# Attention and gated feed-forward on one core: the front as one pinned list of small steps, with the scaling of eight weight conversions on GpSimd

## The chip, the cores and the metric

The kernel runs on one core of a Trainium2 chip. The metric is the device time of one execution in microseconds (us), the median of several runs. TensorE is called PE in the profile (PEld is its weight load), VectorE DVE, ScalarE ACT, GpSimd POOL, and SP is the engine that issues nearly all transfers.

## The reference

```
scores = q @ k.T / sqrt(D);  mask: key at most 63 positions back, none ahead
attn   = exp(scores - max); attn /= (sum + 1e-9)
x      = (attn @ v)   as [4608 tokens, 512]
out    = (sigmoid(x @ w_gate) * (x @ w_val)) @ w_out
```

There are 8 sequences of 576 tokens with 8 heads of 64. The weights are 512x1536, 512x1536 and 1536x512. All is computed to float32 accuracy; the weights arrive as 64-bit numbers, and every product is split in a high and a low part (float32r), three matmuls for one.

## The kernel before

**Tiles.** The 4608 tokens are 12 tiles of 384. A unit of attention is (t, p): tile t and one of 4 pairs of heads p. The hidden width is 12 groups j of 128. Tiles 0 and 1 are computed group by group as the weights come in; tiles 2 to 11 use a scheme with seven products for eight (`product`, `last_product`) and read sums of the weights that are stored to device memory on the way.

**The front.** Before the up-projection of tiles 0 and 1 can run densely, their eight attention units have to be done, since a matmul of the up-projection runs over all four pairs. A unit is: load of q, k (`load_qk`) and v (`load_v`); `scores` (24 matmuls into two PSUM banks, one for each head h of the pair); `softmax`, for each h three pieces u: a DVE operation that adds the mask, scales, negates and finds the lowest value (L249), an exponential on ACT (L257), for h = 0 with a sum in a second ACT instruction; for h = 1 a sum on DVE (L270); then 2(sum + 1e-9) (L264) and its reciprocal (L265) on DVE, and the multiplication by it on GpSimd (L274, 128x384); `stage_b`: three transposes for each h on TensorE (L328) and a copy on ACT (L333); `stage_c`: 24 matmuls with v (L358), high part on ACT (L365), low part on DVE (L366). Then `up_gate` and `up_val` (12 matmuls each, L394), tanh on ACT (L402), the product (L407) and its split on DVE (L420, L422), `down` (L442).

**Weight conversion.** Conversion i is group j = i // 3 of matrix m = i % 3 (gate, val, out). `conv_load` brings 128x512 64-bit numbers (512 KB) to one of six `raw` buffers. `conv_a` scales the high words and the low words, two operations on ACT over every second 32-bit word (L117, L118), the one to a `w32` tile (three buffers), the other in place. `conv_b` puts the float32 together, three operations on DVE (L126, L128, L130). `conv_c` rounds the high part on ACT (L158), takes the low part on DVE (L159), stores parts for the later scheme (`put_part`, `wo_parts`) and the whole `w32` tile (`w32d`).

**Order.** Each piece of work is put into `events` with a time worked out by hand (`put(time, rank, function, ...)`); the events are sorted and traced in that order. The order of the instructions of an engine is then fixed at build time by a scheduler with its own timing; TensorE's keeps the traced order (`pe`). `tc.issue_after(x)` puts an instruction behind x on its engine; conversions use it with `marks` (the last copies of units, the split of a group). Tiles of one tag share its buffers, so a new tile waits until an old one has been read. PSUM banks of the up-projection rotate over three (`h_bank`).

Of the kernel before, what the change touches and what calls it, by code (L numbers as in the profile page):

```python
# [26 lines left out]
def attn_ffn(ctx: ExitStack, tc: tile.TileContext, qT, kT, vN, w_gate, w_val, w_out, out, outT):  # L27
# [74 lines left out]
    def conv_load(i):  # L102
        j, m = divmod(i, KINDS)
        raw = mp.tile([P, DM], I64, name=f"raw_{m}_{j}", tag="raw", bufs=RAW)
        marks["conv_load"] = nc.sync.dma_start(out=raw, in_=w_src[m][J_AT[j]]).ins
        conv[i] = raw

    def conv_a(i):

# [7 lines left out]
        nc.scalar.activation(w32, hw, AF.Copy, scale=2.0 ** -112)  # L117
        nc.scalar.activation(r32, lw, AF.Copy, scale=2.0 ** -29)  # L118
        conv[i] = (r32, w32)

    def conv_b(i):
        j, m = divmod(i, KINDS)
# [3 lines left out]
        nc.vector.tensor_scalar(out=zz, in0=wi, scalar1=4, scalar2=1,  # L126
                                op0=ALU.logical_shift_left, op1=ALU.logical_shift_right)
        nc.vector.scalar_tensor_tensor(out=wi, in0=wi, scalar=-2 ** 31, in1=zz,  # L128
                                       op0=ALU.bitwise_and, op1=ALU.bitwise_or)
        nc.vector.tensor_add(out=wi, in0=wi, in1=r32)  # L130

    def conv_c(i):
        j, m = divmod(i, KINDS)
        _, w32 = conv.pop(i)
# [19 lines left out]
        nc.sync.dma_start(out=w32d[m][J], in_=w32)
        marks[("w", i)] = (cp,)

    def split(w32, hi, lo, eng):
        cp = nc.scalar.copy(hi, w32)  # L158
# [67 lines left out]
    def softmax(t, p):  # L229
        sc = sc_of.pop((t, p))  # L230
        for h in range(2):
            exponentials(t, p, h, sc[h])
            normalize(t, p, h)

    def exponentials(t, p, h, sc):
        g0 = order[t] * UT
# [6 lines left out]
        if h == 0:  # L243
            sums_of[(t, p)] = sm.tile([P, 2, UP], F32, name=f"rs_{t}_{p}", tag="rs")
        rs = sums_of[(t, p)][:, h, :]
        for u in range(UP):
# [2 lines left out]
            nc.vector.tensor_tensor_reduce(out=pt[:, u, :], in0=sc[u], in1=masks[key],  # L249
                                           op0=ALU.add, op1=ALU.min, scale=-SCALE, scalar=3.0e38,  # L250
                                           accum_out=mn[:, u:u + 1])
            with ExitStack() as behind:
                behind.enter_context(table_order())
                if NP * t + p - 2 in marks["pT"] and (t, p) != (1, NP - 1):
                    behind.enter_context(tc.issue_after(marks["pT"][NP * t + p - 2]))
# [1 line left out]
                exp = nc.scalar.activation(pt[:, u, :], pt[:, u, :], AF.Exp, bias=mn[:, u:u + 1],  # L257
                                           scale=-1.0, **sums)
            chain.append(exp.ins)
        st[(t, p, h)] = pt  # L260

    def invert(rs):

        nc.vector.scalar_tensor_tensor(out=rs, in0=rs, scalar=2e-9, in1=rs, op0=ALU.add, op1=ALU.add)  # L264
        nc.vector.reciprocal(out=rs, in_=rs)  # L265

    def normalize(t, p, h):
        pt, rs = st[(t, p, h)], sums_of[(t, p)][:, h, :]
        if t < 2 and h:
            nc.vector.reduce_sum(out=rs, in_=pt, axis=mybir.AxisListType.X)  # L270
# [51 lines left out]

    def stage_b(t, p):
        for h in range(2):
            pt = st[(t, p, h)]
            pp = bank(t, p, f"p{h}", f"pp{h}_{t}_{p}")
            for u in range(UP):
                pe(nc.tensor.transpose(pp[:, u, :], pt[:, u, :], ident))  # L328
            if t < 2:
                pT = mp.tile([P, TT], F32, name=f"pT{h}_{t}_{p}", tag="g", bufs=4).rearrange("p (u c) -> p u c", u=UP)  # L330
            else:
                pT = pt
            cp = nc.scalar.copy(pT, pp)  # L333
            marks["pTv"] = cp.ins
# [27 lines left out]

    def x_split(src, nm, i, eng):
        x2 = xp.tile([P, 2, TT], F32R, name=f"x_{nm}", tag=f"x{i}")
        hi = nc.scalar.copy(x2[:, 0, :], src)  # L365
        lo = eng.tensor_sub(out=x2[:, 1, :], in0=src, in1=x2[:, 0, :].bitcast(F32))  # L366
# [653 lines left out]
```

## Time and profile before

| | |
|---|---|
| median of 3 runs | 947.2 us (946.29 to 947.6) |
| span of the profiled execution, first to last instruction | 945.2 us |
| what the median of the runs has beyond this span | 2.0 us |
| PE busy | 930.8 us, 98% |
| DVE busy | 713.7 us, 76% |
| ACT busy | 501.7 us, 53% |
| POOL busy | 151.2 us, 16% |
| transfers | 273.45 MB, mean 289 GB/s |

The profiled execution is one execution on the chip; its own time is given as the span, so sums are made against that. A row of the timeline gives start, duration, engine, line, operation, output and inputs with shapes, and count; brackets give the idle time in front and what ended it. A group row gives busy time and the mean of one in ns; a source row minimum, median and maximum in ns.

### The profile page before, as it was taken

Reading aid. Unit: us, or ns where it says so; the run is one execution under the profiler, and the core shown is the slowest. Engines: PE = TensorE matmul, PEld = TensorE weight load, DVE = VectorE, ACT = ScalarE, POOL = GpSimd, SP = SyncE. Lnnn points to the kernel's source line nnn. Section 1 sums busy time; section 2 is a strip of 40 time slices with the busy share of each in tenths; the row PEclk is TensorE's granted clock in tenths of the full one; section 3 lists DMA queues with packets and bytes.
Section 4 is the critical chain, followed back from the end, with each engine's and each line's share of the span. In section 5 each row is a group of like instructions: output and inputs, shape, how many; then the busy total and the mean of one; then the engine's idle time right before and its main releaser. Section 6 shows DMA issues by size and latency. Waiting matters only on the chain.

```text
span 945.2 us, 20293 instructions
## 1 busy us (share of the span) xinstructions
PE 930.8 (98%) x7164; PEld 897.2 (95%) x7164; DVE 713.7 (76%) x1919; ACT 501.7 (53%) x1374; POOL 151.2 (16%) x232
## 2 busy tenths in 40 slices
PE   6999999999999999999999999999999999999998
PEld 5899999889999999999999999999999999999998
DVE  7999989887888975666885676796567796566882
ACT  7867676655666653545653255564155555222450
POOL 4201104605683000311100013100011100000000
PEclk9999999999999999999999999999999999999999
DMA  9899998989999989888879888889888688988364
GB/s 339 309 386 366 359 320 283 358 295 352 388 321 314 405 284 294 288 273 270 269 251 312 264 283 293 270 244 288 284 278 280 213 246 281 297 251 256 128 222 158
DMA packets 105509, 273.45 MB, mean 289 GB/s; under 512 B 11456, under 2 KB 33600, under 8 KB 105408
## 3 DMA queue, kind: packets, MB, share of 16 engines
q1 hardware_dynamic: 105408, 272.15, 85.2%
q8 instruction: 57, 0.93, 0.4%
q14 instruction: 44, 0.36, 0.1%
HBM read 220.20 MB, written 51.90 MB: 288 GB/s over the span
## 4 chain that ended last, share of the span: by engine, by line
PE 95%; DVE 2%; DMA 1%; ACT 0%; issue 0%; DVEq 0%; ACTq 0%
PE pr L619 46%; PE y L619 23%; PE ph L394 10%; PE y L442 5%; PE pp L328 3%; PE pr L358 2%; PE s L224 1%; PE oo L358 1%; PE pr L224 1%; DMA wt<-wd 1%; PE s L358 1%; DVE p L249 0%; DVE rs L264 0%; ACT p L257 0%; DVE x L366 0%; DVE rs L270 0%
## 5 line engine op out<-in xcount | busy, mean ns | idle before, releaser
L619 PE MATMUL pr<-x_T,wt 128*128 128x384 f32 x1224 | 224.5, 335 | 0.0
L619 PE MATMUL y<-h,wot 128*128 128x384 f32 x1260 | 219.9, 334 | 0.0
L619 PEld LDWEIGHTS y<-h,wot 128*128 128x128 f32 x1260 | 218.3, 188 | 0.7 <-DVE h L407 0.6
L619 PEld LDWEIGHTS pr<-x_T,wt 128*128 128x128 f32 x1224 | 212.6, 188 | 0.3 <-issue 0.3
L619 PE MATMUL pr<-x_B,wt 128*128 128x384 f32 x1008 | 188.6, 337 | 1.0 <-DMA wt<-wd 1.0
L619 PEld LDWEIGHTS pr<-x_B,wt 128*128 128x128 f32 x1008 | 174.6, 188 | 3.5 <-issue 2.1
L701 ACT CAST h<-h 128x384 fp32r<-128x384 f32 x210 | 104.3, 514 | 91.7 <-PE y L619 41.1
L274 POOL TENSOR_TENSOR p<-p,rs 128x384 f32<-128x384 f32 x76 | 69.3, 926 | 521.7 <-DVE rs L265 243.3
L702 DVE TENSOR_TENSOR h<-h,h 128x384 fp32r<-128x384 f32 x210 | 111.7, 559 | 22.0 <-ACT h L701 21.5
L257 ACT ACTIVATE p<-p,mn 128x128 f32<-128x128 f32 x288 | 110.8, 392 | 20.5 <-DVE mn L249 20.2
L402 ACT ACTIVATE g<-c 128x384 f32<-128x384 f32 x90 | 47.0, 522 | 117.7 <-DVE c L658 117.5
L394 PE MATMUL ph<-x,w 128*128 128x384 f32 x576 | 106.0, 338 | 0.1
L394 PEld LDWEIGHTS ph<-x,w 128*128 128x128 f32 x576 | 99.8, 188 | 2.5 <-issue 0.9
L629 DVE TENSOR_TENSOR c<-pr,p 128x384 f32<-128x384 f32 x60 | 33.0, 550 | 44.5 <-PE pr L619 44.5
L407 DVE SCALAR_TENSOR_TENSOR h<-g,c 128x384 f32<-128x384 f32 x90 | 50.3, 559 | 6.2 <-DVE c L658 0.5
L257 ACT ACTIVATION_READ_ACCUMULATOR p<-p,mn 128x1 f32 x264 | 49.6, 188 | 0.0
L333 ACT COPY p<-pp 128x384 f32<-128x384 f32 x80 | 34.3, 479 | 25.9 <-PE pp L328 23.1
L634 ACT COPY p<-pr 128x384 f32<-128x384 f32 x60 | 27.2, 473 | 37.0 <-PE pr L619 36.9
L629 DVE TENSOR_TENSOR u<-pr,p 128x384 f32<-128x384 f32 x60 | 33.1, 551 | 17.6 <-PE pr L619 17.6
L328 PE MATMUL pp<-ident,p 128*128 128x128 f32 x288 | 41.8, 280 | 2.0 <-POOL p L274 1.9
L619 PE MATMUL pr<-x_T,ws 128*128 128x384 f32 x216 | 40.4, 339 | 0.0
L658 DVE TENSOR_TENSOR c<-pr,p 128x384 f32<-128x384 f32 x60 | 32.9, 554 | 9.6 <-PE pr L619 9.1
(186 smaller groups left out, 1212.1 us busy)
## 6 DMA issues: line engine op xcount, KB each, us to landing
wt<-wd SPq DMA_DIRECT2D x186, 512.0 KB, 4.5
wot<-wod SPq DMA_DIRECT2D x105, 512.0 KB, 4.6
v<-in_vN_dram SPq DMA_DIRECT2D x48, 384.0 KB, 5.5
wd<-ws SPq DMA_DIRECT2D x48, 256.0 KB, 4.9
k<-in_kT_dram SPq DMA_DIRECT2D x48, 224.0 KB, 5.5
q<-in_qT_dram SPq DMA_DIRECT2D x48, 192.0 KB, 5.4
w32d<-w SPq DMA_DIRECT2D x36, 256.0 KB, 4.9
wd<-w SPq DMA_DIRECT2D x36, 256.0 KB, 5.5
```

The lines of the kernel that those rows point to most:

```text
L257: exp = nc.scalar.activation(pt[:, u, :], pt[:, u, :], AF.Exp, bias=mn[:, u:u + 1], scale=-1.0, **sums)
L274: eng.tensor_mul(out=pt, in0=pt, in1=rs.unsqueeze(2).broadcast_to([P, UP, P]))
L328: pe(nc.tensor.transpose(pp[:, u, :], pt[:, u, :], ident))
L358: pe(nc.tensor.matmul(oo[U // 2][h * BLK:(h + 1) * BLK, U % 2 * BLK:(U % 2 + 1) * BLK], vt[:, U, h * BLK:(h + 1) * BLK], pT[h][:, U // 2, ...
L394: pe(nc.tensor.matmul(ph, l, r, start=i == 0, stop=i == len(prs) - 1))
L402: act = nc.scalar.activation(g, c, AF.Tanh)
L407: nc.vector.scalar_tensor_tensor(out=out, in0=g, scalar=1.0, in1=val, op0=ALU.add, op1=ALU.mult)
L442: pe(nc.tensor.matmul(yb[y], l, r, start=first and n == 0, stop=last and n == 2))
L619: pe(nc.tensor.matmul(ps, l, r, start=first and i == 0, stop=last and i == 2, skip_group_check=not check))
L629: marks["plus"] = nc.vector.tensor_add(out=o, in0=ps, in1=a).ins
L701: nc.scalar.copy(h2[:, 0, :], src)
L702: nc.vector.tensor_sub(out=h2[:, 1, :], in0=src, in1=h2[:, 0, :].bitcast(F32))
```

## The change

The functions of the front are cut into steps with names of two letters, each of a few instructions on one engine. A string FRONT lists 333 steps; before all events, they are traced in that order, and every instruction that a step issues through `vector`, `scalar`, `gpsimd` or `sync` keeps its place on its engine. A step that is done is not done again when its event comes (`run`). What is traced for events of a time under 60 is issued behind the last instruction of the list on its engine. The steps: `lq`, `lv`, `cl` loads of q and k, of v, of raw weights; `sc` scores; `tt`, `ex` mask and lowest value, exponential (t.p.h.u); `rd` sum for h = 1; `ia`, `ib` doubled sum, reciprocal; `mu` multiplication; `tr`, `cp` transposes, copy; `ou`, `xh`, `xl` output matmuls, high, low part; `ch`, `cw` scaling of high and low words; `cz`, `cs`, `ca` the three operations of conv_b; `cc`, `cr` high and low part; `ct`, `cd` stores; `ug`, `uv` up-projection matmuls of gate and val; `ut` tanh; `ud` product; `uh`, `ul` its split.

In the list are all eight units, conversions 0 to 7 whole, loads up to conversion 13, loads of units (2,0) and (2,2), both up-projections of (0,0) and (1,0), and the gate matmuls of (0,1). For conversions 0 to 7 `ch` and `cw` run on GpSimd as tensor_scalar; from 8 on they are on ACT as before. The marks that held conversions 0 to 5 behind units are removed.

```
FRONT = """
lq0.0 lq0.1 cl0 lq0.2 sc0.0 lq0.3 cl1 sc0.1 lq1.0 tt0.0.0.2 tt0.0.0.1 ex0.0.0.2 tt0.0.0.0 tt0.0.1.0 ch0 lv0.0
tt0.0.1.2 ex0.0.1.0 tt0.0.1.1 ex0.0.0.0 lq1.1 tt0.1.0.2 cw0 tt0.1.0.0 ex0.0.1.2 tt0.1.0.1 sc0.2 ex0.0.0.1
tt0.1.1.1 tt0.1.1.2 ex0.0.1.1 cl3 ia0.0.0 tt0.1.1.0 ex0.1.1.1 ib0.0.0 cz0 ex0.1.0.0 mu0.0.0 lq1.2 rd0.0.1
sc0.3 ex0.1.0.1 tt0.2.0.0 ex0.1.1.2 ia0.0.1 tt0.2.0.2 ex0.1.1.0 ib0.0.1 tr0.0.0 cs0 ex0.2.0.0 mu0.0.1
ex0.1.0.2 lv0.1 rd0.1.1 ex0.2.0.2 ia0.1.0 tr0.0.1 lv0.3 tt0.2.0.1 cp0.0.0 ib0.1.0 ia0.1.1 tt0.2.1.0 mu0.1.0
ex0.2.0.1 tt0.2.1.1 tt0.2.1.2 sc1.0 cp0.0.1 lq1.3 tt0.3.0.1 tt0.3.0.2 ex0.2.1.2 ch1 tt0.3.0.0 ex0.3.0.2 ou0.0
tt0.3.1.2 tt0.3.1.0 ex0.2.1.1 ca0 cw1 lq2.2 ex0.3.1.0 tr0.1.0 ex0.2.1.0 tt0.3.1.1 sc1.1 ib0.1.1 cp0.1.0 cz1
mu0.1.1 tt1.0.0.0 ex0.3.0.0 rd0.2.1 xh0.0 lv0.2 ch3 tt1.1.0.0 ex0.3.0.1 tr0.1.1 tt1.1.0.2 ex0.3.1.1 tt1.0.0.1
cd0 tt1.0.0.2 cp0.1.1 ia0.2.0 ia0.3.0 ia0.2.1 cz3 ex0.3.1.2 ib0.2.0 ex1.0.0.0 cs1 cl4 ou0.1 mu0.2.0 ex1.0.0.1
tt1.0.1.1 ex1.0.0.2 ib0.2.1 tt1.1.0.1 lv1.1 mu0.2.1 ex1.0.1.1 tt1.0.1.2 tr0.2.0 rd0.3.1 xh0.1 lv1.3 cc0
ib0.3.0 ia1.0.0 ia0.3.1 mu0.3.0 tt1.0.1.0 tr0.2.1 cl2 ex1.1.0.0 ib0.3.1 xl0.0 sc1.2 cp0.2.0 lv1.2 cs3 mu0.3.1
cp0.2.1 lv1.0 tr0.3.0 ex1.1.0.2 xl0.1 cw3 ex1.0.1.0 tr0.3.1 tt1.2.0.2 cp0.3.0 tt1.2.0.1 ou0.2 tt1.2.0.0
cp0.3.1 ib1.0.0 ca1 mu1.0.0 ex1.2.0.0 ou0.3 tt1.2.1.0 ex1.1.0.1 cl6 tt1.2.1.2 tt1.2.1.1 ex1.0.1.2 ia1.1.0 cr0
xh0.2 sc1.3 cd1 cw4 ex1.2.0.2 ib1.1.0 ex1.2.0.1 rd1.0.1 tr1.0.0 xh0.3 mu1.1.0 tt1.1.1.0 lq2.0 xl0.2 ex1.2.1.2
cp1.0.0 tt1.1.1.2 ia1.0.1 cc1 ia1.2.0 tt1.3.0.2 ib1.0.1 xl0.3 ug0.0 ex1.2.1.1 mu1.0.1 ex1.2.1.0 tt1.1.1.1
ex1.1.1.0 tt1.3.0.0 ib1.2.0 tr1.1.0 ex1.1.1.1 cl7 cr1 mu1.2.0 ex1.1.1.2 tr1.0.1 uv0.0 ex1.3.0.0 tt1.3.0.1
rd1.1.1 ch4 ex1.3.0.1 rd1.2.1 ex1.3.0.2 cp1.0.1 tt1.3.1.1 ia1.1.1 ia1.3.0 ut0.0 ib1.1.1 ia1.2.1 cz4 mu1.1.1
ex1.3.1.1 ib1.3.0 tt1.3.1.0 ou1.0 cp1.1.0 tt1.3.1.2 ca3 ex1.3.1.0 mu1.3.0 ex1.3.1.2 tr1.1.1 ib1.2.1 cd3
tr1.2.0 rd1.3.1 mu1.2.1 cp1.1.1 tr1.3.0 cl5 ud0.0 xh1.0 cl9 cc3 ia1.3.1 ib1.3.1 tr1.2.1 cs4 mu1.3.1 ct0
cp1.2.0 ou1.1 cp1.2.1 xl1.0 ca4 cw2 tr1.3.1 cp1.3.0 ou1.2 cr3 cp1.3.1 cd4 ch2 xh1.1 ou1.3 cl10 xh1.2 xl1.1 cw6
cz2 xh1.3 xl1.2 ch6 cc4 xl1.3 ug1.0 cs2 cw7 uh0.0 ca2 uv1.0 ut1.0 cz6 cc2 cd2 cr4 ct1 cs6 ch7 ct3 ug0.1 cr2
lv2.0 cw5 ul0.0 ca6 ch5 cz7 cc6 cd6 cz5 cl8 cs7 cl12 cs5 ct2 ud1.0 ca5 ca7 cc5 cr6 cc7 cd7 cr5 cr7 ct5 cd5
lv2.2 ct6 ct4 cl13 cl11 ct7
"""
```

```diff
+    class Pinned:
+        def __init__(self, eng):
+            self.eng = eng
+        def __getattr__(self, op):
+            def call(*a, **k):
+                ins = getattr(self.eng, op)(*a, **k)
+                if pinned[0]:
+                    tc.keep_in_program_order(ins)
+                    ends[ins.ins.engine] = ins.ins
+                return ins
+            return call
+    vector, scalar, gpsimd, sync = (Pinned(e) for e in (nc.vector, nc.scalar, nc.gpsimd, nc.sync))
+    def run(name, *a):
+        if (name,) + a not in taken:
+            taken.add((name,) + a)
+            steps[name](*a)
...
+    def ch(i):
+        w32 = mp.tile([P, DM], F32, name=f"w32_{m}_{j}", tag="w32", bufs=W32)
+        if i < 8:
+            gpsimd.tensor_scalar(out=w32, in0=hw, scalar1=2.0 ** -112, scalar2=None, op0=ALU.mult)
+        else:
+            scalar.activation(w32, hw, AF.Copy, scale=2.0 ** -112)
...
+    def cw(i):
+        if i < 8:
+            gpsimd.tensor_scalar(out=r32, in0=lw, scalar1=2.0 ** -29, scalar2=None, op0=ALU.mult)
+        else:
+            scalar.activation(r32, lw, AF.Copy, scale=2.0 ** -29)
...
     events.sort(key=lambda x: (x[0], x[1]))
+    pinned[0] = True
+    for token in FRONT.split():
+        run(token[:2], *map(int, token[2:].split(".")))
+    pinned[0] = False
     for tm, _, f, a in events:
-        if f in (conv_a, conv_b, conv_c):
-            with ExitStack() as behind:
+        with ExitStack() as behind:
+            for ins in ends.values() if tm < 60 else ():
+                behind.enter_context(tc.issue_after(ins))
+            if f in (conv_a, conv_b, conv_c):
...
-                key = j - AHEAD if m < 2 else j - 1
-                early = {3: ("1_1",), 2: ("1_3",), 4: ("1_3",), 5: ("1_3",)}.get(a[0], (key,))
+                early = (j - AHEAD if m < 2 else j - 1,)
...
-                if a[0] < 2:
-                    behind.enter_context(tc.issue_after(marks["pT"][a[0] + (f is conv_c)]))
```

More of the change, by code (lines that the diff above doesn't have):

```diff
@@ L141, in conv_c @@
             w2 = wo_all[j][:, j % 2]
-        J = J_AT[j]
         if m == 2:
@@ L233, in softmax, with mask_of, lowest @@
             normalize(t, p, h)
-    def exponentials(t, p, h, sc):
-        g0 = order[t] * UT
+    def mask_of(t, u, h):
+        key = [int((order[t] * UT + 2 * u + s) % SEQ == 0) for s in range(2)]
+        return masks[tuple(key[::-1] if h else key)]
+    def lowest(t, p, h):
         if t < 2 and (NP * t + p) % 3 == 2:
@@ L321, in stage_n, with tr, cp @@
             normalize(t, p, h)
+    @step
+    def tr(t, p, h):
+        pt = st[(t, p, h)]
+        pp = pp_of[(t, p, h)] = bank(t, p, f"p{h}", f"pp{h}_{t}_{p}")
+        for u in range(UP):
+            pe(nc.tensor.transpose(pp[:, u, :], pt[:, u, :], ident))
+    @step
+    def cp(t, p, h):
+        pp = pp_of.pop((t, p, h))
+        if t < 2:
+            pT = mp.tile([P, TT], F32, name=f"pT{h}_{t}_{p}", tag="g", bufs=4).rearrange("p (u c) -> p u c", u=UP)
+        else:
+            pT = st[(t, p, h)]
+        marks["pTv"] = scalar.copy(pT, pp).ins
+        if t < 2:
+            marks["pT"][NP * t + p] = marks["pTv"]
+        st[(t, p, h)] = pT
@@ L323, in stage_b @@
     def stage_b(t, p):
         for h in range(2):
[L325 to L334, printed above, removed]
@@ L335, in stage_b, with ou, xh @@
-            if t < 2:
-                marks["pT"][NP * t + p] = cp.ins
-            st[(t, p, h)] = pT
+            run("tr", t, p, h)
+            run("cp", t, p, h)
+    @step
+    def ou(t, p):
+        oo = oo_of[(t, p)] = bank(t, p, "o", f"oo_{t}_{p}")
+        outputs(t, p, [oo[:, u, :] for u in range(UP)])
+    @step
+    def xh(t, p):
+        oo = oo_of[(t, p)].rearrange("p u c -> p (u c)")
+        if t < 2:
+            x2 = xs[(t, p)] = xp.tile([P, 2, TT], F32R, name=f"x_{t}_{p}", tag=f"x{4 * t + p}")
+            marks[f"{t}_{p}"] = (scalar.copy(x2[:, 0, :], oo).ins,)
+        else:
+            marks["xf"] = scalar.copy(xf_tile(t, p), oo).ins
@@ L339, in stage_c, with xl @@
+    @step
+    def xl(t, p):
+        oo = oo_of.pop((t, p)).rearrange("p u c -> p (u c)")
+        x2 = xs[(t, p)]
+        lo = vector.tensor_sub(out=x2[:, 1, :], in0=oo, in1=x2[:, 0, :].bitcast(F32))
+        marks[f"{t}_{p}"] += (lo.ins,)
     def stage_c(t, p):
-        oo = bank(t, p, "o", f"oo_{t}_{p}")
-        outputs(t, p, [oo[:, u, :] for u in range(UP)])
-        oo = oo.rearrange("p u c -> p (u c)")
+        run("ou", t, p)
+        run("xh", t, p)
         if t < 2:
-            xs[(t, p)] = x_split(oo, f"{t}_{p}", 4 * t + p, nc.vector)
-        else:
-            marks["xf"] = nc.scalar.copy(xf_tile(t, p), oo).ins
+            run("xl", t, p)
```

243 lines of the change are left out of this document (169 added, 74 removed).

## The prediction

> **What bounds the kernel now.** I read the page's engine totals first, then busy time by stretch, then what ended TensorE's waits, and last the front in order of time.
>
> ```profile
> span 945.2 us, 20293 instructions
> PE 930.8 (98%) x7164; PEld 897.2 (95%) x7164; DVE 713.7 (76%) x1919; ACT 501.7 (53%) x1374; POOL 151.2 (16%) x232
> 5.60:34.70 29.10, 24.58 (x348) 19.78 (x348) 26.18 (x146) 26.28 (x95) 13.19 (x15) 1.00 1.02 387
> 34.70:40.30 5.60, 4.78 (x86) 3.99 (x85) 4.86 (x11) 4.18 (x10) 0.83 (x1) 1.00 0.60 228
> 40.30:180.00 139.70, 139.70 (x1041) 130.25 (x1040) 129.01 (x323) 98.28 (x248) 34.38 (x49) 1.00 0.96 343
> 40.30 8.79 PE L394 MATMUL ph<-x,w 128*128 128x384 f32 x48
> ```
>
> (Columns of a stretch: its length, then busy us and count of PE, PEld, DVE, ACT, POOL, granted clock, DMA share, GB/s.) TensorE is idle for 14.4 us in all, and from 40.30 to 180 not at all. Only the first 40.3 us can give anything: call D the start of the 48 up-projection matmuls at 40.30 (two for tile 1, group 0, two for tile 0, group 1). Ahead of D both kernels must do the same TensorE work, all eight attention units and both halves of up(0,0); so the gain is 40.30 minus the new D (the start of ug1.0), less any stall that the new order causes behind it. From 5.6 to 34.7 DVE (26.18 of 29.10) and ACT (26.28) are both about 90% busy: two co-bounds, with DMA full as well.
>
> **Does taking work off ACT move the end?** Rows that give start-to-start times, which is what an engine in a row of work pays:
>
> ```profile
> 21.10 0.42 DVE L126 TENSOR_SCALAR zz<-w 128x512 int32<-128x512 int32 x1
> 21.44 0.17 DVE L265 RECIPROCAL rs<-rs 128x3 f32<-128x3 f32 x1
> 21.56 0.69 DVE L128 SCALAR_TENSOR_TENSOR w<-w,zz 128x512 int32<-128x512 int32 x1
> 22.17 0.55 DVE L366 TENSOR_TENSOR x<-oo,x 128x384 fp32r<-128x384 f32 x1
> 22.64 0.85 DVE L130 CUSTOM_DVE_ANT_0 w<-raw,w 128x1024 uint16<-128x1024 uint16 x1
> ...
> 27.38 0.52 DVE L270 TENSOR_REDUCE rs<-p 128x3 f32<-128x384 f32 x1
> 27.82 0.28 DVE L249 CUSTOM_DVE_ANT_0 p<-s,m 128x128 f32<-128x128 f32 x1
> 28.02 0.08 DVE L249 DVE_READ_ACCUMULATOR2_ANT mn<- 128x1 f32 x1
> ...
> 21.54 0.40 ACT L257 ACTIVATE p<-p,mn 128x128 f32<-128x128 f32 x1
> 21.93 0.40 ACT L257 ACTIVATE p<-p,mn 128x128 f32<-128x128 f32 x1
> 18.41 0.61 ACT L158 CAST w<-w 128x512 fp32r<-128x512 f32 x1
> 18.92 0.67 ACT L117 ACTIVATE w<-raw 128x512 f32<-128x512 f32 x1
> 36.65 0.69 ACT L117 ACTIVATE w<-raw 128x512 f32<-128x512 f32 x1
> 37.23 0.66 ACT L118 ACTIVATE raw<-raw 128x512 int32<-128x512 uint32 x1
> 37.79 1.61 ACT L333 COPY pT<-pp 128x384 f32<-128x384 f32 x4
> ```
>
> DVE: tt 0.21 (0.28 long, the next 0.20 to 0.21 behind it), rd 0.44, xl 0.47, cz 0.34, cs, ca and cr 0.61 each, ib 0.1, ia 0.08. ACT: an ex that also sums 0.39, cc 0.51, a pair ch, cw 1.14. Before, three pairs (conversions 0, 1, 3) lie ahead of D on ACT, 3.4 us, one of them at 36.65 in front of the last copies. They go; on ACT alone D could come 3.4 earlier. But DVE gets more: by rd1.3.1, the last sum, the list has cz, cs, ca, cr 4, 3, 3, 2 times where before had 2 each: 2 x 0.34 + 2 x 0.61 = 1.9 more, less one xl (0.47): 1.4 net. So DVE decides, and with it what it shares with GpSimd:
>
> ```profile
> 26.41 0.83 POOL L274 TENSOR_TENSOR p<-p,rs 128x384 f32<-128x384 f32 x1 [1.64 <-DVE rs L265]
> 26.60 0.65 DVE L264 SCALAR_TENSOR_TENSOR rs<-rs 128x3 f32<-128x3 f32 x1
> 21.78 1.16 POOL L274 TENSOR_TENSOR p<-p,rs 128x384 f32<-128x384 f32 x1 [1.97 <-ACT p L257]
> L264 DVE SCALAR_TENSOR_TENSOR rs<-rs x16: 149/162/666, 7.2 to 35.3; 128x3 f32<-128x3 f32 x16
> L264 DVE SCALAR_TENSOR_TENSOR rs<-rs 128x3 f32<-128x3 f32 x16 | 4.5, 280 | 1.0 <-ACT p L257 0.8
> ```
>
> A 0.16 us DVE operation (median) begun under a GpSimd multiply lasts 0.65 and ends with it, at 27.25 against 27.24; the multiply at 21.78 lasts 1.16 instead of 0.83 because cs at 21.56 has the way. So DVE operations with two SBUF inputs (ia, cs, ca, cr) and GpSimd exclude one another; tt, xl (one input in PSUM) and rd pass. Before, this cost L264 4.5 - 16 x 0.16 = 1.9 us. I count cz, which no row shows under a multiply, as excluded too. The short operation needs its 0.16, so it was let in at 27.09, 0.15 before the multiply's end.
>
> The Trainium skill, "SBUF — State Buffer", section "SBUF: two separate sides", calls the shared port pair an exclusive lock held for the full instruction; the trace agrees on the exclusion, but shows the 0.15 of early release.
>
> **Price X of a scaling on GpSimd** (128x512, one input). No row has it. The nearest:
>
> ```profile
> L274 POOL TENSOR_TENSOR p<-p,rs x76: 825/831/1274, 7.8 to 738.1; 128x384 f32<-128x384 f32 x76
> L543 POOL TENSOR_TENSOR sw<-sw,a x24: 448/460/911, 156.0 to 285.3; 128x128 f32<-128x128 f32 x24
> masks.py:199 POOL TENSOR_SCALAR_AFFINE_SELECT ident<-ident 128x128 f32<-128x128 f32 x1 | 0.3, 342 | 0.1
> masks.py:197 POOL MEMSET ident<- 128x128 f32 x1 | 0.2, 204 | 0.1
> L1005 POOL MEMSET const-float32-0.0<- 128x1 f32 x1 | 0.1, 98 | 0.2 <-issue 0.2
> ```
>
> Two inputs: (825 - 448)/256 = 1.47 ns an element over 0.26 fixed, 1.01 us at 512. No input: (204 - 98)/127 = 0.83 ns over 0.10, 0.53. One input lies between: X = 0.8. Upper end 1.37, the 342 ns of 128 elements scaled by four; lower end 0.53.
>
> The Trainium skill, "GPSIMD Engine Reference", section "3.1 Elementwise — side-by-side cycle accounting", has 512 elements at 1.8 cycles each as 769 ns; with 0.77 the walk below would end 0.15 earlier.
>
> **The walk.** Rows for its start and its end:
>
> ```profile
> 5.61 0.29 DVE L249 CUSTOM_DVE_ANT_0 p<-s,m 128x128 f32<-128x128 f32 x1 [2.46 <-PE s L224]
> 6.57 2.84 PE L224 MATMUL s<-k,q 64*64 64x128 f32 x48 [1.11 <-DMA k<-in_kT_dram]
> ...
> 31.01 0.92 PE L358 MATMUL oo<-pT,v 128*64 128x64 f32 x24
> 34.74 0.54 DVE L270 TENSOR_REDUCE rs<-p 128x3 f32<-128x384 f32 x1
> ```
>
> The pinned list fixes each engine's order. Read with GpSimd's steps as posts, it has a pattern: behind a GpSimd step stand DVE steps that pass (tt, rd, ib, xl), and the excluded ones come after them. So I take each GpSimd step and the passing DVE steps side by side, then the excluded DVE steps, let in 0.15 before GpSimd ends. DVE starts at 5.61, when sc0.0 is done.
> - Start: four tt to 6.45. ch0 waits for raw 0, now the third load pair: 1.38 MB, which the front's 363 to 390 GB/s brings by about 7.0; ch0, cw0 to 8.6. tt0.1.* need sc0.1, half of the 48 matmuls at 6.57, so 8.0: a 1.1 us hole behind the sixth tt. DVE at cz0's end 9.8, cs0's 11.5.
> - Unit 1 to 3: mu0.0.1 with rd and ia, 12.8; mu0.1.0 with four tt, 13.7; ch1 with three tt, then ca0, 14.9; cw1, then cz1, 15.9; mu0.1.1, 16.7; ch3 with four tt, then 3 ia, cz3, ib, cs1, 18.7.
> - mu0.2.0 and mu0.2.1 to 20.3; mu0.3.0 then cs3, 21.7; mu0.3.1 with xl0.1, 22.4; cw3 with three tt, then ca1, 23.8; mu1.0.0 with three tt, then cr0, 25.1.
> - cw4 with rd, 25.9; mu1.1.0 with tt, xl, 2 ia and more, 27.5; mu1.0.1 then cr1, 28.6; mu1.2.0, 29.4; ch4, then ia and cz4, 30.8; mu1.1.1 then ca3, 32.1; mu1.3.0 with rd1.3.1, 32.8; mu1.2.1 with ud0.0, then ia, ib, cs4, 34.3; mu1.3.1 to 35.1.
> - Then as in the rows before: tr1.3.1 0.5, cp 0.45, ou1.3 1.0 (24 matmuls, 0.92) with hops of 0.05 to 0.1: 37.4, where ug1.0 starts, its last x half (xh 0.46, xl 0.55: 38.4) being needed only 1.6 later.
>
> So the last rd begins near 32.2 instead of 34.74, and from there to D it is 5.2 instead of 5.56. The walk has no hops between dependent steps of one engine. Calibrated on before: until 34.74 DVE has 48 tt 10.1, 7 rd 3.1, ia and ib 2.7, 5 xl 2.35, two conversions 4.3 = 22.5, 1.9 excluded, 2.9 idle: 27.3 of 29.1, 1.8 in hops. The list mostly puts another step between ia and ib and between cz, cs and ca, so I take a third, 0.6. **D = 38.0, 2.3 earlier.**
>
> **Other parts.** ACT in the list up to xh1.3: 24 ex of 0.39, 24 of 0.29, 16 cp of 0.37, 8 xh of 0.36, three cc of 0.51, one ut of 0.4 = 27.1 from 5.95, so 33.1 against 37.4: covered, by 4 us. Loads: the last v, lv1.0, stands behind 9.5 MB.
>
> ```profile
> w32d<-w SPq DMA_DIRECT2D x4, 256.0 KB, 5.6
> 51.01 2.27 PE L394 MATMUL ph<-x,w 128*128 128x384 f32 x12
> ```
>
> At 387 GB/s after the 1 MB of the first 5.6 us that is 28 us, and ou1.0 stands at about 29; the chain behind it needs 5, so it would bind only past 32. On SP, cd0 is now ahead of cl4 and six v loads, but it is the 26th issue and ca0 is done at 14.9; cd3, behind ca3 at 32.1, holds back cl5 and cl9 alone, which nothing ahead of D uses.
>
> Behind D the list pins conversions 5 to 7 ahead of everything else. ug1.1 (D + 10.7, as 51.01 is to 40.30 now) needs the PSUM bank of uv1.0, freed by ud1.0. On DVE ud1.0 stands behind cs2, uh, ca2, cz6, cr4, cs6, cr2, ul, ca6, cz7, cz5, cs7, cs5: 7.0 from D + 1. But ch5 needs conversion 2's w32 buffer, whose store is issued after ca2 (D + 2.9) and lands 5.6 later (row): ch5 ends at D + 9.3, ud1.0 at D + 11.4, a stall of 0.7; a landing 0.7 sooner, and none. I take 0.2. The removed waits of conversions on marks cost nothing, the list replaces them.
>
> Sum: 40.30 - 38.0 - 0.2 = 2.1 off the profiled span of 945.2, so 943.1; the median stands 2.0 above that span, for what lies around it: 945.1, rounded to **945.0**.
>
> **Rivals.**
> - *GpSimd's price.* X = 1.37 lengthens six groups where the scaling is longer than its cover (ch1, cw1, ch3, cw3, cw4, ch4): from 4.8 to 8.2, D 41.4, 948.5, slower; with X at 1.15 nothing is gained. For it: stride of two words and a uint32 input, in no row. Against: the two-input rate gives 1.01. At 0.53 D comes 0.9 earlier, 944.1.
> - *The bank.* If the w32 store lands 2 us later than its median, in a queue that runs full, the stall is 2.5 and the gain is gone: 947.3.
> - *The port is held to the very end.* Nine groups wait 0.15 more: D 39.4, 946.4. The early release is seen only on a short operation.
> - *No hop and no hole:* DVE's steps up to xl1.3 alone sum to 29.1; from 5.6, with the 1.1 hole, D would be 34.9 and the time 941.8, if every exclusion fell into idle time.
> - *ACT was the bound after all:* the 3.4 us come off whole, 943.8.
>
> The held lock is the rule named above from "SBUF — State Buffer" of the Trainium skill.
>
> **Chances.** Forecast, 943.0 to 946.0: 0.47, three quarters of it by over 0.2%. Better (no hop and no exclusion paid, 941.5 to 943): 0.12; ACT as the bound would lie in the forecast's own range. Gain eaten by bank or lock, 945.5 to 948.5: 0.21 (the lock alone 0.06). GpSimd's price at its upper end or above, or a late load: 0.20, nearly all slower. Of 947.2, 0.2% is 1.9 us, about what a measurement can tell: faster 0.47, same 0.34, slower 0.19. Range: from the case without holes, 941.5, to the upper X with a 1 us stall behind it, 949.5.
>
> **What would show it.** Right: GpSimd's scalings near 0.8, at most 0.2 over; ACT idle between copies before D, DVE over 90% busy from 8 on; L264's successor (ia) near its 0.16 median with few at 0.65; D at 38 and TensorE without a gap behind. Wrong: scalings over 1.1; cs, ca, cr stretched beyond 0.7 all along; TensorE waiting at ug1.1 for DVE; a first tt of unit 1 later than 8, or ou1.0 waiting for a v load.

## The result and the profile after

The changed kernel took 957.3 us (median, 955.6 to 959.6) where the kernel before took 947.4 on the same chip: a ratio of 1.0105, interval 1.0091 to 1.0118, 9.9 us slower. The profiled execution of the changed kernel has a span of 955.1 (before 945.2), the same 9.9. The forecast was 945.0, with 949.5 as its upper end.

Below, the rows of the kernel before that the prediction does not show (timeline of TensorE, then a group by operation from 5.5 to 57 us: busy us, mean ns of one, idle in front). Y, the first matmul of the first `down`, stands right behind the 48 dense matmuls and marks their end cleanly: an effective D is Y minus 8.63 (48.93 - 40.30). It counts pauses inside the 48 matmuls as well.

```profile
48.93 0.63 PE L442 MATMUL y<-w,hh 128*128 128x512 f32 x2
83.80 0.81 PE L328 MATMUL pp<-ident,p 128*128 128x128 f32 x6
180.53 0.88 PE L224 MATMUL s<-k,q 64*64 64x128 f32 x22 [0.22 <-ACT xf L346]
...
L159 DVE TENSOR_TENSOR w<-w,w 128x512 fp32r<-128x512 f32 x7 | 4.8, 687 | 1.1 <-ACT w L158 1.1
```

The changed kernel: busy time of two stretches (columns as in the prediction), two of the things that TensorE waited for up to 200 us (total, times, longest), GpSimd's groups up to 70 us, and TensorE's rows that answer to those of before. All pinned steps have one line, L125, so they are told apart by their tiles.

```profile
5.60:34.70 29.10, 22.91 (x321) 18.17 (x321) 24.55 (x141) 23.35 (x87) 24.29 (x20) 1.00 1.00 379
34.70:42.28 7.58, 5.86 (x112) 4.61 (x111) 7.32 (x17) 5.08 (x14) 5.72 (x7) 1.00 0.55 151
...
PE pp L490 <- POOL p L125: 3.9, 7, 1.0
PE oo L546 <- ACT pT L125: 0.6, 1, 0.6
...
L125 POOL TENSOR_TENSOR p<-p,rs 128x384 f32<-128x384 f32 x16 | 14.9, 948 | 2.7 <-DVE rs L125 1.7 <-ACT p L125 0.7
L125 POOL TENSOR_SCALAR raw<-raw 128x512 int32<-128x512 uint32 x8 | 14.7, 1839 | 0.6
L125 POOL TENSOR_SCALAR w<-raw 128x512 f32<-128x512 f32 x8 | 12.3, 1544 | 5.7 <-DMA raw<-in_moe_w_gate_dram 5.4
...
42.28 1.51 PE L574 MATMUL ph<-x,w 128*128 128x384 f32 x7
44.67 7.40 PE L574 MATMUL ph<-x,w 128*128 128x384 f32 x41 [0.88 <-DVE x L125]
51.91 0.63 PE L650 MATMUL y<-w,hh 128*128 128x512 f32 x2
56.77 2.38 PE L574 MATMUL ph<-x,w 128*128 128x384 f32 x12 [2.62 <-DVE h L125]
90.52 2.35 PE L574 MATMUL ph<-x,w 128*128 128x384 f32 x12 [1.89 <-ACT g L125]
92.71 0.71 PE L490 MATMUL pp<-ident,p 128*128 128x128 f32 x5
189.54 0.88 PE L341 MATMUL s<-k,q 64*64 64x128 f32 x22 [0.22 <-ACT xf L125]
```

GpSimd did 24.3 us of work in the stretch up to 34.7 where it had 13.2 before. It starts only at 9.07, so it is busy for 95% of the 25.6 us that are left, while DVE (24.6, before 26.2) and ACT (23.4, before 26.3) were busy for less of the same stretch: up to 34.7 GpSimd is the fullest engine. From 34.70 to 42.28 it is DVE again, 7.32 of 7.58 us. The granted clock is 1.00 in both stretches, as before. The two scalings take 1.54 and 1.84 us, 27.0 in all for sixteen. Read down the landmarks, the 9.9 us come in three portions. At Y it is 3.0 (51.91 against 48.93), an effective D of 43.3; ug1.0 itself starts at 42.28, and 1.0 us of pauses follows inside the 48 matmuls, 0.88 of it waiting for the last x half (xl1.3). At ug1.1 it is 5.8 (56.77 against 51.01), behind the wait at 90.52 it is 8.9 (92.71 against 83.80). From there to 189.54 nearly nothing is added (9.0), and 0.9 more by the end.

The stall at ug1.1, 2.6 us, in the rows of GpSimd and DVE in front of it:

```profile
40.17 1.93 POOL L125 TENSOR_SCALAR raw<-raw 128x512 int32<-128x512 uint32 x1
...
53.07 1.52 POOL L125 TENSOR_SCALAR w<-raw 128x512 f32<-128x512 f32 x1
...
54.62 0.43 DVE L125 TENSOR_SCALAR zz<-w 128x512 int32<-128x512 int32 x1 [2.25 <-POOL w L125]
56.17 0.55 DVE L125 SCALAR_TENSOR_TENSOR h<-g,ph 128x384 f32<-128x384 f32 x1
```

From 40.17 to 54.59 GpSimd does the last eight scalings (cw2 to ch5) without a pause; cz5 waits for ch5, ud1.0 (56.17) stands behind cz5 in DVE's order, and the PSUM bank of ug1.1 is freed by ud1.0. No store is in this chain.

### The profile page after: what moved, and what is told of

It reads as the page before. It is cut to its first block, busy times and chain, and to the rows that moved or that the text cites. A ratio compares the mean times of both kernels' runs of the same rounds, so it can differ in the third digit from the quotient of the medians.

```text
span 955.1 us, 20284 instructions
## 1 busy us (share of the span) xinstructions
PE 931.4 (98%) x7164; PEld 896.1 (94%) x7164; DVE 715.1 (75%) x1919; ACT 492.3 (52%) x1358; POOL 179.9 (19%) x248
## 4 chain that ended last, share of the span: by engine, by line
PE 84%; DMA 6%; DVE 4%; POOL 2%; issue 1%; ACT 1%; SPq 0%; DVEq 0%; POOLq 0%; ACTq 0%
PE pr L827 44%; PE y L827 23%; PE ph L574 7%; PE pp L490 3%; PE pr L546 2%; PE y L650 2%; PE s L341 1%; DMA wd<-ws 1%; DVE w L125 1%; POOL p L125 1%; PE pr L341 1%; DMA wd<-w 1%; DMA w32d<-w 1%; POOL w L125 1%; DMA raw<-in_moe_w_val_dram 1%
## 5 line engine op out<-in xcount | busy, mean ns | idle before, releaser
L436 POOL TENSOR_TENSOR p<-p,rs 128x384 f32<-128x384 f32 x60 | 55.2, 937 | 494.3 <-PE pr L827 231.2
L125 ACT ACTIVATE g<-c 128x384 f32<-128x384 f32 x90 | 47.0, 522 | 117.3 <-DVE c L866 99.4
L419 ACT ACTIVATE p<-p,mn 128x128 f32<-128x128 f32 x240 | 93.5, 392 | 17.3 <-DVE mn L414 17.2
L837 DVE TENSOR_TENSOR c<-pr,p 128x384 f32<-128x384 f32 x60 | 33.1, 551 | 44.0 <-PE pr L827 44.0
L125 DVE SCALAR_TENSOR_TENSOR h<-g,c 128x384 f32<-128x384 f32 x90 | 50.4, 560 | 6.2 <-ACT p L125 0.5
L125 ACT COPY p<-pp 128x384 f32<-128x384 f32 x80 | 34.3, 479 | 26.3 <-PE pp L490 26.3
L837 DVE TENSOR_TENSOR u<-pr,p 128x384 f32<-128x384 f32 x60 | 33.1, 551 | 17.9 <-PE pr L827 17.9
L419 ACT ACTIVATION_READ_ACCUMULATOR p<-p,mn 128x1 f32 x240 | 45.1, 188 | 0.0
L490 PEld LDWEIGHTS pp<-ident,p 128*128 128x128 f32 x288 | 34.1, 142 | 9.4 <-POOL p L125 6.7
```

The source lines that it names most:

```text
L125: ins = getattr(self.eng, op)(*a, **k)
L436: eng.tensor_mul(out=pt, in0=pt, in1=rs.unsqueeze(2).broadcast_to([P, UP, P]))
L837: marks["plus"] = nc.vector.tensor_add(out=o, in0=ps, in1=a).ins
```

## The experiments

Two theories. *Price*: a scaling on GpSimd costs twice what the forecast took, and with it GpSimd sets D and ud1.0. *Tail*: the list pins conversions 5 to 7 ahead of everything else, and that loses time behind D whatever a scaling costs. A third, that the list is a gain at a fair price, is the forecast's own. The texts recorded before the runs call Price theory A, and the list's own cost theory B or, for the tail, C.

**The price by itself.** Behind the last output of the kernel before, GpSimd runs scalings, a copy and multiplications on scratch tiles, with nothing beside them.

```diff
+    for o, x in (...):   # f32/u32 in, f32/i32 out, contiguous or every second word; 512, 256, 128
+        nc.gpsimd.tensor_scalar(out=o, in0=x, scalar1=2.0 ** -29, scalar2=None, op0=ALU.mult)
+    nc.gpsimd.tensor_copy(out=r_con, in_=f_con)
+    nc.gpsimd.tensor_mul(out=r_con, in0=f_con, in1=f_con)
```

> The kernel before with a list of GpSimd operations behind its end, each twice, on 128 x n of scratch data, nothing else running: what a scaling costs by form. If the element count alone sets the price: 1.5 us for 512 contiguous float32, 0.75 for 256, 0.4 to 0.5 for 128. If the stride of two words does: about 0.8 contiguous against 1.5 strided. If the conversion does: uint32 to int32 0.3 above float32 to float32 (1.84 against 1.53).

Its rows (timeline of GpSimd; the second and the sixth read every second word):

```profile
920.29 1.49 POOL L989 TENSOR_SCALAR bench_out<-bench_in 128x512 f32<-128x512 f32 x1
921.87 1.53 POOL L989 TENSOR_SCALAR bench_out<-bench_in 128x512 f32<-128x512 f32 x1
926.32 0.85 POOL L989 TENSOR_SCALAR bench_out<-bench_in 128x256 f32<-128x256 f32 x1
927.25 0.53 POOL L989 TENSOR_SCALAR bench_out<-bench_in 128x128 f32<-128x128 f32 x1
934.77 1.49 POOL L989 TENSOR_SCALAR bench_out<-bench_in 128x512 int32<-128x512 uint32 x1
937.92 1.56 POOL L989 TENSOR_SCALAR bench_out<-bench_in 128x512 int32<-128x512 uint32 x1
941.18 0.61 POOL L990 COPY bench_out<-bench_in 128x512 f32<-128x512 f32 x1
941.88 1.04 POOL L991 TENSOR_TENSOR bench_out<-bench_in 128x512 f32<-128x512 f32 x1
```

(1.49 - 0.85)/256 and (0.85 - 0.53)/128 are both 2.5 ns an element. The stride adds 0.07 at most (1.56 against 1.49); the conversion from uint32 to int32 takes the same 1.49. So the price is the plain price of a tensor_scalar, set by the number of elements, the first of the three cases above; a multiplication with two inputs is cheaper, 1.04, and the 1.01 that the prediction worked out for it was close.

**The list without GpSimd.** All scalings stay on ACT; ch0 stands ahead of cz0 and cw0 ahead of ib0.1.0 in the list.

```diff
-        if i < 8:
-            gpsimd.tensor_scalar(out=w32, in0=hw, ...)      # and the same for r32
+        if False:
```

> The pinned list as it is, but all scalings on ScalarE as before (ch0 moved to just ahead of cz0, cw0 to ahead of ib0.1.0, so that ScalarE does not wait for the first raw load). Theory A, the price of a scaling on GpSimd (1.53 us for ch, 1.84 for cw in the changed kernel against the 0.8 of the forecast): with the price gone the list is bounded by ScalarE, 5.9 us of start + 27.1 + 11 scalings of 0.57 = 39.3, so the dense start lies at 39.5 to 41.5 and there is no stall behind it: 946.5 to 949. Theory B, the pinned order itself is worse than the scheduler's: the dense start stays near 43 and the tail stalls: 953 or more.

Measured 949.8, ratio 1.0020 (1.0008 to 1.0031), span 947.7.

```profile
50.38 0.63 PE L651 MATMUL y<-w,hh 128*128 128x512 f32 x2
```

The time lies between the two expectations, 0.8 above the range of theory A. Effective D is 41.8, 1.5 later than before, with the scalings where they had always been. In this execution TensorE's granted clock was 0.50 from 22.5 to 25.9, which may be part of the 1.5; the three executions at a mean clock of 1.000 took 948.7 to 950.1, so the loss in time is there without it. Against the changed kernel it is 7.5 us faster (949.8 against 957.3): GpSimd's part of the loss is about three quarters, the list's own a quarter.

**GpSimd without the list.** The kernel before, with both scalings of conversions 0 to 7 on GpSimd.

```diff
-        nc.scalar.activation(w32, hw, AF.Copy, scale=2.0 ** -112)    # and r32
+            nc.gpsimd.tensor_scalar(out=w32, in0=hw, scalar1=2.0 ** -112, scalar2=None, op0=ALU.mult)
```

> The kernel before, no list, with both scalings of conversions 0 to 7 on GpSimd; the scheduler orders the rest. Theory A (price): conversions 2 and 4 must pass GpSimd at 3.4 us a pair right when the up-projections of group 1 want them, so TensorE stalls behind the dense start and the time is 950 to 956. Theory B (list): within 1.5 us of the kernel before, 946 to 949.

Measured 962.2, ratio 1.0158 (1.0141 to 1.0175), span 960.2. The waits of TensorE up to 200 us, Y, and TensorE's granted clock in slices of 24 us (tenths; 9 is 90% or more):

```profile
PE pp L332 <- POOL p L278: 13.0, 8, 3.7
63.33 0.63 PE L446 MATMUL y<-w,hh 128*128 128x512 f32 x2
...
PEclk8599999999999999999999999999999999999999
```

The loss is larger than either expectation, and it lies in the front, not behind it: Y is 14.4 late. Here the transposes wait 13.0 us for multiplications that stand behind scalings on GpSimd. TensorE's granted clock was also 0.50 from 18.4 to 45.7 (1.00 in the fronts of the kernel before and of the changed kernel), and TensorE was busy for 44.9 us up to Y where the kernel before needed 39.6. So the 14.4 are not GpSimd's waits alone, and the run does not price the scalings by itself. The list has fewer of these waits (3.9 us in 7); it does not cause them.

**Half of it on GpSimd.** In the list, ch on GpSimd as in the change, cw on ACT (cw0 ahead of ib0.1.0).

```diff
-        if i < 8:
-            gpsimd.tensor_scalar(out=r32, in0=lw, ...)
+        if False:
```

> The list with ch on GpSimd and cw on ScalarE (cw0 moved to ahead of ib0.1.0). GpSimd's added time is then 8 x 1.53 = 12.2 us, about what the forecast had counted for all sixteen (12.8). Theory A: the walk of the forecast, corrected for raw 0 landing at 9.07 instead of 7.0 (0.9) and for three ch of 1.53 under covers of 0.63 to 0.84 (2.1), less the cw no longer there (0.75), gives a dense start at 40.2 and at most 0.5 of stall: 946.5 to 949. Theory B: 952 or more.

Measured 951.4, ratio 1.0031 (1.0013 to 1.0049); the profiled execution was below that median, 949.5, span 947.7.

```profile
48.11 0.63 PE L651 MATMUL y<-w,hh 128*128 128x512 f32 x2
50.99 2.35 PE L575 MATMUL ph<-x,w 128*128 128x384 f32 x12 [0.63 <-DVE h L126]
83.10 2.38 PE L575 MATMUL ph<-x,w 128*128 128x384 f32 x12 [1.15 <-ACT g L126]
```

The dense stage begins 0.8 earlier than before and the kernel is still slower: what is won at Y is lost at ug1.1 and at 83. The median falls between the two expectations. The two waits fit the tail, at half the price; no run at this price without the tail shows it.

**At the forecast's price.** The list as changed, but ch is a multiplication with a broadcast constant (1.04 alone) and cw a copy of zeros (0.61 for a contiguous float32 copy alone): 0.83 in the mean. The low words of weights 0 to 7 are left out of the result.

```diff
-            gpsimd.tensor_scalar(out=w32, in0=hw, scalar1=2.0 ** -112, scalar2=None, op0=ALU.mult)
+            gpsimd.tensor_mul(out=w32, in0=hw, in1=k112.broadcast_to([P, DM]))
-            gpsimd.tensor_scalar(out=r32, in0=lw, scalar1=2.0 ** -29, scalar2=None, op0=ALU.mult)
+            gpsimd.tensor_copy(out=r32, in_=k29.broadcast_to([P, DM]))
```

> The changed kernel with both GpSimd steps made cheaper: ch as a multiplication of two inputs (by a constant, broadcast; 1.04 us in the list of prices), cw as a copy of zeros (0.61), which leaves the low words of conversions 0 to 7 out of the weights. A mean of 0.83, the price that the forecast took. Theory A, the price alone was wrong: the dense start comes to 38 to 39.5 (the raw load landing later than the forecast had it adds up to 1.1), the stall at ug1.1 shrinks below 1 us, 945 to 947.5. Theory C, the pinned list itself delays what follows (its last steps hold back everything behind them): the dense start comes early all the same, but 2 to 4 us are lost behind it, 948 to 951.

Measured 949.6, ratio 1.0022 (1.0012 to 1.0032); the profiled execution was the fastest of its runs, 947.7, span 945.9.

```profile
L129 POOL TENSOR_TENSOR w<-raw,k 128x512 f32<-128x512 f32 x8 | 9.6, 1197 | 7.7 <-DMA raw<-in_moe_w_gate_dram 5.0 <-DMA w32d<-w 2.7
L129 POOL COPY raw<-k 128x512 int32<-128x512 int32 x8 | 7.0, 879 | 0.0
47.99 0.63 PE L654 MATMUL y<-w,hh 128*128 128x512 f32 x2
50.85 2.36 PE L578 MATMUL ph<-x,w 128*128 128x384 f32 x12 [0.61 <-DVE h L129]
```

The price alone moves Y by 3.9 us, from 51.91 to 47.99, and the stall at ug1.1 from 2.6 to 0.6. Effective D is 39.4, 0.9 earlier than before. In place the two cost 1.04 in the mean, against 1.69 in the changed kernel: 3.9 us of effective D for 0.65 us of price, six to one. Counted at the start of ug1.0 itself (42.28 and 39.06) it is 3.2 us, five to one. The time is what theory C expected: an early front, and what it wins lost behind it.

**The tail out of the list.** The changed kernel with conversions 5 and 7 and the loads cl13 and cl11 taken out of the list; those two are scaled on ACT at their events' place.

```diff
-...ch7 ...cw5 ...ch5 cz7 ...cz5 ...cs7 ...cs5 ...ca5 ca7 cc5 ...cc7 cd7 cr5 cr7 ct5 cd5 ...cl13 cl11 ct7
-        if i < 8:
+        if i < 8 and i not in (5, 7):
```

> The changed kernel with conversions 5 and 7 (and two loads that need their buffers) taken out of the list, ordered by the scheduler and scaled on ScalarE; the rest of the list and its GpSimd price as they are. Dense start unchanged (43.3 in effect). Theory C: the stall of 2.6 at ug1.1 and those of 0.7 and 1.9 behind it go, 952 to 954.5. Theory A alone (all of it is the price, before the dense start): at most 1 us better, 956 or more.

Measured 951.5, ratio 1.0046 (1.0030 to 1.0062); the profiled execution was the slowest of its runs, 953.8, span 952.0.

```profile
53.16 0.63 PE L650 MATMUL y<-w,hh 128*128 128x512 f32 x2
```

Y is 4.2 late in this execution, whose granted clock was 0.50 from 24.0 to 27.4, and ug1.1 follows at 55.24 without a wait. Two conversions fewer in the list bring 5.9 us in the medians (957.3 to 951.5), a little more than theory C expected. From Y to the end of the span the kernel before takes 896.3 us, the changed kernel 903.2 and this one 898.8: of the 6.9 us that are lost behind Y, 4.4 go with the two conversions. Where the other 1.5 of the medians lie, this one execution does not show.

**Cheap high words, complete result.** In the list, cw on ACT and ch as the multiplication; once with the whole list, once with conversions 5 and 7 out of it as above.

> The list with cw on ScalarE and ch on GpSimd as a multiplication of two inputs, 1.04 us instead of 1.53; all weights complete. Theory A: half a microsecond for each of the three ch under short cover, dense start 38.2 to 39.2 against 39.7 with ch as a scaling, and the time 1 to 1.5 below that kernel, 948 to 950. Theory C: the dense start comes earlier by as much, the time does not follow in full.

> The same with conversions 5 and 7 out of the list (scaled on ScalarE, ordered by the scheduler). Theories A and C together: dense start 38.2 to 39.2 and nothing lost behind it: 945 to 946.5, faster than the kernel before. Theory A alone: within 0.5 of the kernel with ch as a multiplication and the whole list.

Measured 947.8, ratio 1.0005 (0.9996 to 1.0014), and 947.7, ratio 1.0000 (0.9991 to 1.0010). Y of the first, then of the second:

```profile
48.69 0.63 PE L653 MATMUL y<-w,hh 128*128 128x512 f32 x2
```

```profile
48.85 0.63 PE L652 MATMUL y<-w,hh 128*128 128x512 f32 x2
```

Both stand within 0.25 of the kernel before at Y, an effective D of 40.1 and 40.2, about 1 us above the range expected, and cannot be told from it in time. The second was expected to be faster than the kernel before if the tail cost something whatever the price; it met the expectation of theory A alone instead. With a scaling of 1.25 instead of 1.73 on GpSimd, and only one for each conversion, the tail costs nothing that shows: its cost goes with GpSimd's work in it.

**Loads of the start.** The second of these, with the first two raw loads behind q and k of tile 0 (cl0 ahead of lq1.0, cl1 ahead of lq1.1; ch0, cz0, cs0 some steps back).

> The list with cw on ScalarE, ch on GpSimd as a two-input multiplication, conversions 5 and 7 out of the list (that kernel gave 947.7, up-projection start 40.2), and now the two first raw loads moved behind all q and k loads of tile 0 (cl0 behind lq0.3, cl1 behind lq1.0), with ch0, cz0 and cs0 moved some steps back to match. There the scores of unit 1 start at 7.3 instead of 6.6 in the kernel before, with 4.0 and 1.75 us of waiting for k. If the early raw loads cost the front its start: unit 1's scores start by 6.7, the dense start comes to 39.0 to 39.6 and the time falls to 946.3 to 947.2. If DVE's order is what limits (rival): the start comes earlier, but the dense start stays at 40.0 to 40.4 and the time at 947.4 to 948.2.

Measured 949.3, ratio 1.0016 (1.0006 to 1.0026).

```profile
6.36 4.05 PE L343 MATMUL s<-k,q 64*64 64x128 f32 x59 [0.53 <-DMA k<-in_kT_dram]
49.52 0.63 PE L652 MATMUL y<-w,hh 128*128 128x512 f32 x2
```

The scores of unit 1 start at 6.4, a microsecond sooner, as the first expectation wants, and Y comes 0.7 later than without the move. Neither expectation met the figure: moving the raw loads back brought nothing. What takes the 0.7 is not shown. Conversion 0 begins later, but the granted clock was also 0.50 from 14.4 to 17.9 in this execution and 1.00 in the one without the move; of this kernel's eleven executions the two at a mean clock of 1.000 took 947.7 and 949.5, the four at 0.994 to 0.997 took 949.6 to 951.4.

**The forecast's price and no tail.** The kernel at the forecast's price, with conversions 5 and 7 out of the list (those two are scaled on ACT).

> The list with ch as a two-input multiplication and cw as a copy of zeros on GpSimd (the low words of weights 0 to 4 and 6 are left out of the result), a mean price of 0.83 alone, and conversions 5 and 7 out of the list. With them in the list this gave 949.6 at a dense start of 39.3, with 0.6 and 1.3 us of waiting behind it. If what is lost behind the dense start is the tail of the list alone, the waits behind it go and the time is 945.9 to 946.8, about 1 us under the kernel before, which is all that the front at the forecast's price is worth. If the losses behind it have another cause (every later conversion held behind the list), the time stays at 948.5 to 949.8. The forecast's own figure, 945.0, would need a dense start at 38.0.

Measured 948.1, ratio 0.9999 (0.9989 to 1.0008), span 946.7.

```profile
48.18 0.63 PE L654 MATMUL y<-w,hh 128*128 128x512 f32 x2
50.26 2.27 PE L578 MATMUL ph<-x,w 128*128 128x384 f32 x12
83.59 0.82 PE L494 MATMUL pp<-ident,p 128*128 128x128 f32 x6
```

The stall at ug1.1 is gone and the time lies between the two expectations. The lead of 0.75 at Y and ug1.1 (50.26 against 51.01) is 0.2 at 83.59 (against 83.80) and gone at 180.68 (against 180.53). A wait of 0.27 is part of this; the rest is in no wait of the trace, and what takes it stays open. With the tail in the list the same prices gave 949.6, so there the tail costs 1.5 to 2 us (949.6 against 948.1, 1.0022 against 0.9999). One more thing separates the executions of this kernel: the three at a mean granted clock of 1.000 took 945.9 to 946.2, the eight at 0.997 to 0.999, the profiled one among them (0.50 from 20.0 to 23.4), 946.7 to 949.2. The kernel before, beside them, took 947.0 in the median of eleven executions at 1.000 and 947.6 in that of ten below. So without the lower clock the front may be worth the 1 us that the first expectation gave it; three executions do not show it.

## Why the prediction was wrong, step by step

**The step that failed: the price.** "One input lies between: X = 0.8." It rested on the guess that a tensor_scalar, with one input, costs something between an operation with none and one with two. It costs 1.49 to 1.56 alone, above the two-input multiplication (1.04) and above the stated upper end, 1.37; in place 1.54 and 1.84. The only row of a one-input operation, 342 ns for 128 elements or 2.7 ns an element, had been used for the upper end alone; the measured slope is 2.5 ns, over a fixed part of 0.2 us. That row should have pulled the value up, and the range of X should have ended above it. In the sum, the span came out 12.0 us above the 943.1 of the forecast: 5.3 in D (43.3 for 38.0), 2.6 at ug1.1 (2.8 lost there for a term of 0.2), and 4.1 behind it, for which the sum had no term.

**The walk with the right price.** The rival "GpSimd's price" named the mechanism: six groups that grow with X. With the 1.69 measured in place, 38.0 + 6 x (1.69 - 0.8) = 43.3, and the effective D is 43.3; the two lists that differ in price alone give the same six. So the walk had the direction and about the size of the price's effect. The agreement to the tenth is luck. The D of the prediction is the start of ug1.0, and that came at 42.28: the other 1.0 is pauses behind it, 0.88 of it for xl1.3, which the walk had counted as covered. The six scalings themselves took 1.64 in the mean, which gives 43.1. And the early posts were off. These rows of the changed kernel are the scores of unit 1, the first scaling and the first tt of unit 1:

```profile
7.48 1.56 PE L341 MATMUL s<-k,q 64*64 64x128 f32 x24 [2.02 <-DMA k<-in_kT_dram]
9.07 1.52 POOL L125 TENSOR_SCALAR w<-raw 128x512 f32<-128x512 f32 x1 [5.41 <-DMA raw<-in_moe_w_gate_dram]
9.08 0.29 DVE L125 CUSTOM_DVE_ANT_0 p<-s,m 128x128 f32<-128x128 f32 x1 [2.23 <-PE s L341]
```

Raw 0 was used at 9.07, not 7.0, and unit 1 began at 9.08, not 8.0. The forecast let 1.38 MB pass at the front's 363 to 390 GB/s. The transfers moved 61 GB/s up to 2.5 us and 311 from there to 9.07, which is 2.2 MB by then, and 1.38 MB by about 6.5. So the rate is not what was late: loads issued behind raw 0 were moved beside it before it had landed.

**"DVE decides."** At 1.69 it does not decide alone: up to 34.7 GpSimd is the fuller engine, and DVE, whose operations last longer beside the scalings, is full only from there to 42.28. That ACT is covered held: TensorE waits 0.6 us for it ahead of D. With all scalings back on ACT the same list is 1.5 late at D.

**The bank.** The place was right (ug1.1 behind ud1.0 behind cz5 behind ch5), the cause and the size were not: 0.2 was taken, 2.6 came, and what was late was GpSimd, not the store of conversion 2. At the forecast's price the stall is 0.6, inside its 0 to 0.7, and there a w32 store does hold GpSimd up, by 2.7 us. Neither the wait at 90.52 nor any other loss behind ug1.1 was in the sum: the tail of the list puts cc5 and cc7 ahead of tanh on ACT, and later conversions behind both. In the changed kernel's rows of ACT:

```profile
57.35 1.22 ACT L125 CAST w<-w 128x512 fp32r<-128x512 f32 x2 [5.12 <-DVE w L125]
58.48 0.48 ACT L125 ACTIVATE g<-ph 128x384 f32<-128x384 f32 x1
```

ACT stands idle for 5.12 us in its pinned order, waiting for cc5 and cc7, before it gets to the tanh at 58.48. That the wait at 90.52 comes from the same tail is inferred: with conversions 5 and 7 out of the list it is gone.

**The exclusion.** Right against the multiplications, wrong against the scalings. The prediction lets no DVE operation with two SBUF inputs run beside any GpSimd step. An ia begun under a multiplication still lasts to its end (0.64 at 27.74, the multiplication from 27.54 to 28.37), but five of them ran inside scalings in 0.13 to 0.16. The larger cr4 (w<-w,w) also begins and ends inside one scaling, and each of the two takes longer for it. These are the rows, and DVE's groups from 5.5 to 57 us:

```profile
47.41 1.81 POOL L125 TENSOR_SCALAR raw<-raw 128x512 int32<-128x512 uint32 x1
47.71 1.14 DVE L125 TENSOR_TENSOR w<-w,w 128x512 fp32r<-128x512 f32 x1
...
L125 DVE TENSOR_TENSOR w<-w,w 128x512 fp32r<-128x512 f32 x5 | 5.0, 1008 | 0.0
L125 DVE TENSOR_SCALAR zz<-w 128x512 int32<-128x512 int32 x8 | 4.6, 581 | 5.1 <-POOL w L125 5.1
L125 DVE SCALAR_TENSOR_TENSOR rs<-rs 128x3 f32<-128x3 f32 x16 | 3.3, 229 | 0.0
```

The low part (w<-w,w) grew to 1008 ns and zz to 581, against 687 before and the 0.42 us of the row in the prediction, and GpSimd's own operations grew too (its multiplication by the sums is 948 ns in the mean, 876 before). ia (rs<-rs) fell from 280 only to 229, not near 0.16. zz, which was counted as excluded without a row, is held by a multiplication (1.05 us at 34.88) and passes beside scalings, in 0.43 to 0.88. So the walk let DVE wait and GpSimd run on; beside a scaling DVE need not wait, and both pay.

**The rest.** The loads of v ahead of D did not bind, as said: no wait of TensorE for v stands in the changed kernel's list of waits. Even with operations of the forecast's price the gain at Y is 0.9 and not 2.3; the price in place was 1.04 rather than 0.8, which at six to one is the difference. And the gain did not reach the end. So 945.0 would not have come with X = 0.8 alone either: the term "less any stall behind it" was sized by one stall.

## What to carry to other kernels

Before work is moved to an engine that has no row for it, run that operation there by itself: a price guessed by interpolation between other operations was off by a factor of two and carried the whole sum. Multiply its error by the number of groups in which the moved step sets the pace (five to six here), and make the range that wide. A pinned order also pins what stands behind it, so add up what waits at its end as carefully as what it brings forward.

## What the runs showed of the hardware

GpSimd's tensor_scalar on 128x512 takes 1.49 us alone, its tensor_tensor 1.04 and its copy 0.61: the operation with one tensor and one scalar is the dearest of the three. Reading every second word adds at most 0.07, uint32 to int32 nothing. The Trainium skill, "GPSIMD Engine Reference", section "3.1 Elementwise — side-by-side cycle accounting", gives two inputs about 2.6 cycles an element and the best case, a tight loop over 512 elements, 769 ns; it has no figure for a tensor_scalar. Here the operation with one tensor input is dearer than the one with two, and the measurement decides.

Beside DVE work, both sides stretch: the copies of zeros took 0.65 to 1.18 in the front, 0.88 in the mean, the scalings of low words 1.84 instead of 1.56, and DVE's low part 1.01 instead of 0.69. The low part at 47.71 ran whole inside the scaling at 47.41, and ia inside five scalings took 0.13 to 0.16, where inside a multiplication it lasted 0.32 to 0.64: GpSimd's multiplication of two tensors held it up, its tensor_scalar did not.

TensorE's granted clock was 0.50 for 3.4 us in the front of four profiled executions (from 22.5, 24.0, 14.4 and 20.0 us), at no common place of the list, and for 27.3 us in the one of GpSimd without the list.
